# The gate products of a two-MLP attention kernel in Strassen's form

## The chip, the cores and the metric

The kernel runs on one core of a Trainium2 chip. The metric is device time in microseconds of a whole execution. The profile is of one such execution; its own time stands in the table below, beside the median of the runs.

## The reference

Attention on 4 x 8 heads of 576 tokens and 64 columns, half of the heads with a plain window of 32, half with a window dilated by 4, is laid out as 2,304 tokens of 512 columns and goes through two MLPs:

```
h  = x @ w_in                     # 2304 x 512 @ 512 x 2048
y  = maximum(0.01 * h, h) @ w_out # 2304 x 2048 @ 2048 x 512
a  = y @ w1;  b = y @ w2          # 2304 x 512 @ 512 x 1024, twice
out = ((a * b) @ w3) @ w_out2     # 1024 x 1024, then 1024 x 512
```

The inputs are float64 arrays, passed as 64-bit words. The change concerns the two products `y @ w1` and `y @ w2`, their elementwise product and the last product.

## The kernel before

**Number form.** Every matmul operand is kept as two float32r parts, high and low, and a product is three matmuls of 128 x 128 weights (`mm3`, L118 to L122: low x high, high x low, high x high). `split` (L109 to L116) makes the parts: a cast on one engine, a subtraction on another. Weights come as 64-bit words; `Convert` (L170) loads 512 KB of them at a time, forms float32 words in five passes (`to_float32`, L144: a scaling on an engine of choice, two passes of ScalarE, a shift and a word sum of VectorE), and hands them to a finisher that splits them into a slot.

**Stages.** Attention fills `xs`. The first MLP runs in turns: `hidden_steps` makes one block of 128 hidden columns for a chunk of tokens (12 matmuls into a bank `ps_h`), the activation follows on ScalarE, `split` on VectorE (and GpSimd), and `project_steps` multiplies the block into four sums `ps_x` (12 matmuls), two turns later (`LAG = 2`, L897). There are 7 chunks of 16 turns, 112 in all; the last ones have 384 tokens. A finished chunk is copied from PSUM into `st_t` (L491) and stored to `x2_dram` (L579). Meanwhile `w3 @ w_out2` is folded into one matrix, 1024 x 512, kept in `wp_dram` (`fold_steps` L635, `store_steps` L644): 32 fold steps whose `w_out2` parts are stored once and read back.

**Order.** Up to turn 96 the order on every engine is written out by hand: `START` (L794) is read one letter at a time, each letter issuing one step (H, g, c, l: a hidden turn; J: its projection; digits and d: conversions of the fold; W: a fold step), `LOADS` names the load behind each L. What follows is issued by loops, and the tile framework orders it: of the instructions that its own timing model has ready on an engine, the one issued first goes first. So TensorE's order after turn 96 may differ from the loops', while waits and queues still hold each engine to the order found. All loads and stores are issued by the sync engine, in one queue.

**Gate and last product.** In the last chunk's 16 turns (L912 to L949) the 16 column blocks of w1 and w2 are converted and split into the 16 slots `win` that the first MLP's weights leave; the folded matrix is loaded and split into `wo` slots (`load_wp`, `split_wp`). Then (L960 to L970) y is taken in blocks of 256, 512, 512, 512 and 512 tokens. `gate` makes, for one block of 128 columns, both products (24 matmuls), copies the first out of PSUM, multiplies, and splits the result into a `p` slot. `final` multiplies 128 tokens of `p` with the folded matrix (24 matmuls of 512 columns) and stores 256 KB of the result; it is issued among the gate steps of the next token block. `split_y` prepares a block of y during the block before it.

PSUM has three tags: `acc`, two pairs of banks (`bank2`), `side`, two banks (`side_bank`), and `h`, two banks (`bank`).

Of the kernel before, what the change touches and what calls it, by code (L numbers as in the profile page):

```python
# [8 lines left out]
F32 = mybir.dt.float32  # L9
# [19 lines left out]
def tile_window_attention_two_mlps(  # L29
# [30 lines left out]
    TB = 512  # L60
    GATE = [(0, T % TB)] + [(t, TB) for t in range(T % TB, T, TB)]
    NCB = len(GATE)
# [105 lines left out]
    LAST_CONV = ("GAD",)  # L168
# [40 lines left out]
    win, wout, w12, wo2, wp = {}, {}, {}, {}, {}  # L209
# [443 lines left out]
    yf, ys, pr = {}, {}, {}  # L653

    def load_y(c):
        t0, n = GATE[c]
        t = (fin if c else first_y).tile([P, NC, n], F32, tag="yf", name=f"yf{c}", bufs=1)
        nc.sync.dma_start(t, x2_dram[:, t0 : t0 + n].rearrange("(e p) t -> p e t", p=P))
        yf[c] = t

    wpf = {}

    def load_wp(ib):
        t = late.tile([P, DM], F32, tag="wpf", name=f"wpf{ib}", bufs=2)
        nc.sync.dma_start(t, wp_dram[ib * P : (ib + 1) * P, :])
        wpf[ib] = t

    def split_wp(ib):
        t = wo_slot(f"wps{ib}")
        split(t[:, 0], t[:, 1], wpf.pop(ib), nc.scalar, nc.gpsimd)  # L670
        wp[ib] = t

    def split_y(c, cc):
        if cc == 0:
            ys[c] = (fin if c else first_y).tile(
                [P, 2, NC, GATE[c][1]], F32R, tag="ys", name=f"ys{c}", bufs=2 if c else 1
            )
        t = ys[c]
        split(
            t[:, 0, cc], t[:, 1, cc], yf[c][:, cc], nc.scalar,  # L680
            nc.gpsimd if cc % 2 else nc.vector,
        )

    def gate(c, i):
        y, n = ys[c], GATE[c][1]
        if c == i == 0:
            ps = [side_bank(f"ps_ab{c}_{i}_{m}") for m in range(2)]
        else:
            both = bank2(f"ps_ab{c}_{i}")
            ps = [both[:, m] for m in range(2)]  # L690
        for m in range(2):
            for cc in range(NC):
                mm3(
                    ps[m][:, :n], parts(w12[m, i], cc), parts(y, cc), cc == 0, cc == NC - 1
                )
        t = fin.tile([P, TB], F32, tag="a", name=f"a{c}_{i}", bufs=2)[:, :n]
        nc.scalar.copy(t, ps[0][:, :n])  # L697
        g = fin.tile([P, TB], F32, tag="ab", name=f"ab{c}_{i}", bufs=2)[:, :n]
        nc.vector.tensor_tensor(g, t, ps[1][:, :n], op=ALU.mult)  # L699
        gg = fin.tile([P, 2, TB], F32R, tag="p", name=f"p{c}_{i}", bufs=NI + 4)[:, :, :n]  # L700
        split(gg[:, 0], gg[:, 1], g, nc.scalar, nc.gpsimd)
        pr[c, i] = gg

    def final(c, tb, pieces=1):
        r0 = GATE[c][0] + tb * P
# [17 lines left out]
    with ExitStack():  # L723
# [40 lines left out]
        PAIR_AT = "VVKVKVKVKVKVKVKVKVKVKVVVKKVKKKKV"  # L764
# [13 lines left out]
        for f in range(NF + AHEAD):  # L778
# [29 lines left out]
            "d2d13L2Jg3L45c645lH60J1dg02cd1lLH23453L645Jg6clH01d0Jgd2c1lL23H453L645J6gclH01d02dJg"
            "3L1c45l2H6L345Jg6L0Lc1dlLH20L31d4gJ5c2l6L3LW4LW56HL0Wg1dc0J2Ll1L32dWL34L45656WWL01dW"
            "L02H1dL3L23L4gW5cl6JeLf4W5061dWL021dWL3L243LH5L6JgclW01dHL23L4gW05c61lJL2d3LWHL4gJ05"  # L810
            "c61l2dWiL3jHkLmWgclJeLf4H5061d2Wg3LcJlLWHL4gW05c61lJL2d3LHWgclJL4W5061dHL23LWgclJL4H"
            "5061d2Wg3cJlLWHeLf4gJ05c61l2dW3HLWgclJL4W56HLJgclWHL4gW5cl6JWHJgclWHWgclJefHJgclHJgc"
            "l"
# [3 lines left out]
            "yyyyyyyyyyzzzyyzzzzyyzzzzyyzzyzzyzyzyzyzzyzzzyzzyzzzzzzz"  # L817
# [91 lines left out]
        turn = len(begun["Hgcl"][-1]) - 1  # L909
        first = turn + 1  # L910
        for c, f0, f1 in runs:
            if first >= f1 - f0:  # L912
                first -= f1 - f0
                continue
            f0, first, f00 = f0 + first, 0, f0
            if c == NCH - 1:
                fold_es.close()
                first_es, first_y = pool("first", "right")
                late_es, late = pool("late", "right")

                def raw_last(i):
                    return late.tile([P, 512], U64, tag="raw", name=f"raww{i}", bufs=2)

                wr = {}

                def w_slot(i):
                    wr[i] = late.tile([P, 2, 512], I32, tag="wr", name=f"wr{i}", bufs=2)
                    return wr[i][:, 0]

                jobs = [  # L930
                    (load_cols, (w1, w2)[m], i, keep_cols(w12, (m, i), f"w{m + 1}_{i}"))
                    for i in range(NI)
                    for m in range(2)
                ]
                conv = Convert(jobs, raw_last, w_slot, lambda i: wr[i][:, 1], LAST_CONV)
                conv.fetch(2)
                load_y(0)
            for f in range(f0, f1):
                turn += 1
                mlp1(c, f, f00, f1)  # L940
                lagged()
                if c == NCH - 1:
                    conv.step()
                    if 2 <= f < 2 + NI:
                        load_wp(f - 2)
                    if 3 <= f < 3 + NI:
                        split_wp(f - 3)
                    if 11 <= f < 11 + NC:
                        split_y(0, f - 11)  # L949
        while todo:  # L950
            project(*todo.pop(0))
        conv.step()

        gs_es.close()
        xs_es.close()
# [51 lines left out]
```

## Time and profile before

| | |
|---|---|
| median of 3 runs | 856.58 us (852.99 to 859.01) |
| profiled execution | 854.51 us, of which the span from first to last instruction is 852.7 us |
| granted TensorE clock | 1.00 of full speed in every slice |
| TensorE (PE) busy | 839.7 us, 98% of the span, 5,778 matmuls |
| VectorE (DVE), ScalarE (ACT), GpSimd (POOL) | 342.9, 351.1, 200.5 us: 40, 41, 24% |
| moved by DMA | 103.58 MB, 121 GB/s over the span; packets 40% of the 16 engines' time |
| gate and last product | from about 551.6 us to 849.6 us |

Engine names in the rows are those in brackets; PEld is TensorE's weight load, SPq the sync engine's queue. A group line reads: line, engine, operation, out<-in, shapes, count, busy us, mean ns of one, idle time before, and what ended it. Matmul durations overlap; their price is the distance between starts.

### The profile page before, as it was taken

The page shows a single profiled execution, that of the slowest core. Times are in us where ns is not written, and L with a number is a line of the kernel's source. Part 1 is how long each engine was busy: PE and PEld are TensorE (multiplying, and loading weights), DVE is VectorE, ACT ScalarE, POOL GpSimd, SP SyncE. Part 2 cuts the span into 40 slices and gives each one's busy share as a digit, 9 for nine tenths or more (in the row PEclk, how much of TensorE's full clock was granted, in tenths as well). Part 3 has the DMA queues.
Part 4 walks back from the last instruction along what each step waited for, and adds up shares of the span by engine and source line. Part 5 has one row for each costly group of instructions (what it writes and reads, how often), then busy time and mean ns, then how long its engine had stood idle before and what let it go on. Part 6 is the DMA issues. An engine that isn't in the chain of part 4 may idle for free.

```text
span 852.7 us, 14709 instructions
## 1 busy us (share of the span) xinstructions
PE 839.7 (98%) x5778; PEld 771.0 (90%) x5778; DVE 342.9 (40%) x705; ACT 351.1 (41%) x884; POOL 200.5 (24%) x230
## 2 busy tenths in 40 slices
PE   8899999999999999999999999999999999999998
PEld 7799999999999999889999999998888888888887
DVE  4799995246355346443321478631020010000000
ACT  4899874124545456453221465442121122111111
POOL 3210110132323234322221334142131131111110
PEclk9999999999999999999999999999999999999999
DMA  6985977134364037896643464141001000000001
GB/s 144 273 279 168 260 182 181 47 83 112 86 155 105 20 105 281 324 328 235 213 158 100 151 194 155 56 139 60 13 6 64 18 13 13 26 12 13 25 13 49
DMA packets 87332, 103.58 MB, mean 121 GB/s; under 512 B 42848, under 2 KB 65632, under 8 KB 87264
## 3 DMA queue, kind: packets, MB, share of 16 engines
q1 hardware_dynamic: 87264, 102.65, 39.8%
q8 instruction: 45, 0.74, 0.4%
q14 instruction: 23, 0.19, 0.1%
HBM read 85.72 MB, written 16.91 MB: 120 GB/s over the span
## 4 chain that ended last, share of the span: by engine, by line
PE 90%; DMA 4%; SPq 2%; DVE 1%; issue 1%; ACT 1%; POOL 0%; ACTq 0%; POOLq 0%; DVEq 0%
PE ps_h L120 8%; PE ps_x L120 8%; PE ps_x L122 7%; PE ps_x L121 7%; PE ps_ab L120 7%; PE ps_ab L121 7%; PE ps_ab L122 7%; PE ps_h L122 7%; PE ps_h L121 7%; PE ps_y L121 4%; PE ps_y L122 4%; PE ps_y L120 4%; PE ps_s L380 2%; PE ps_wp L120 2%; PE ps_wp L121 2%; PE ps_wp L122 2%
## 5 line engine op out<-in xcount | busy, mean ns | idle before, releaser
L120 PE MATMUL ps_h<-x,win 128*128 128x384 f32 (+2 forms) x448 | 143.3, 320 | 0.2
L122 PE MATMUL ps_h<-x,win 128*128 128x384 f32 (+2 forms) x448 | 140.0, 312 | 0.0
L121 PE MATMUL ps_h<-x,win 128*128 128x384 f32 (+2 forms) x448 | 139.9, 312 | 0.0
L699 DVE TENSOR_TENSOR ab<-a,ps_ab 128x512 f32<-128x512 f32 (+1 forms) x40 | 25.4, 634 | 233.5 <-ACT a L697 224.2
L120 PE MATMUL ps_ab<-ys,w 128*128 128x512 f32 (+1 forms) x320 | 117.7, 368 | 0.2 <-DVE ab L699 0.2
L122 PE MATMUL ps_ab<-ys,w 128*128 128x512 f32 (+1 forms) x320 | 117.7, 368 | 0.0
L121 PE MATMUL ps_ab<-ys,w 128*128 128x512 f32 (+1 forms) x320 | 117.6, 368 | 0.0
L120 PE MATMUL ps_x<-gs,wout 128*128 128x384 f32 (+2 forms) x356 | 114.1, 321 | 0.0
L122 PE MATMUL ps_x<-gs,wout 128*128 128x384 f32 (+2 forms) x356 | 112.4, 316 | 0.0
L121 PE MATMUL ps_x<-gs,wout 128*128 128x384 f32 (+2 forms) x356 | 112.3, 316 | 0.0
L505 ACT ACTIVATE g<-ps_h 128x384 f32<-128x384 f32 (+2 forms) x112 | 49.1, 439 | 135.5 <-PE ps_h L122 116.2
L112 POOL TENSOR_TENSOR p<-ab,p 128x512 fp32r<-128x512 f32 (+1 forms) x40 | 47.0, 1177 | 210.7 <-ACT p L110 210.7
L112 POOL TENSOR_TENSOR gs<-g,gs 128x384 fp32r<-128x384 f32 (+2 forms) x64 | 58.4, 914 | 154.2 <-DVE gs L110 154.2
L120 PEld LDWEIGHTS ps_h<-x,win 128*128 128x128 f32 x448 | 84.5, 189 | 2.9 <-PE ps_o L454 0.2
L121 PEld LDWEIGHTS ps_h<-x,win 128*128 128x128 f32 x448 | 84.6, 189 | 0.6
L122 PEld LDWEIGHTS ps_h<-x,win 128*128 128x128 f32 x448 | 84.5, 189 | 0.0
L110 DVE CAST gs<-g 128x384 fp32r<-128x384 f32 (+2 forms) x89 | 34.3, 386 | 120.7 <-ACT g L505 101.6
L697 ACT COPY a<-ps_ab 128x512 f32<-128x512 f32 (+1 forms) x40 | 21.7, 544 | 137.4 <-PE ps_ab L122 137.4
L120 PEld LDWEIGHTS ps_ab<-ys,w 128*128 128x128 f32 x320 | 60.1, 188 | 10.7 <-DVE ab L699 0.6
L121 PEld LDWEIGHTS ps_ab<-ys,w 128*128 128x128 f32 x320 | 60.1, 188 | 10.1
L122 PEld LDWEIGHTS ps_ab<-ys,w 128*128 128x128 f32 x320 | 60.1, 188 | 9.9
L120 PEld LDWEIGHTS ps_x<-gs,wout 128*128 128x128 f32 x356 | 67.1, 189 | 1.4
(108 smaller groups left out, 1567.4 us busy)
## 6 DMA issues: line engine op xcount, KB each, us to landing
wo<-wo_dram SPq DMA_DIRECT2D x32, 512.0 KB
raw<-in_moe_w_in_dram SPq DMA_DIRECT2D x16, 512.0 KB
raw<-in_moe_w_out_dram SPq DMA_DIRECT2D x16, 512.0 KB
rawf<-in_moe_w_dram SPq DMA_DIRECT2D x16, 512.0 KB
raww<-in_moe_w_dram SPq DMA_DIRECT2D x16, 512.0 KB
q<-in_q_dram SPq DMA_DIRECT2D x48, 140.0 KB
k<-in_k_dram SPq DMA_DIRECT2D x48, 140.0 KB
v<-in_v_dram SPq DMA_DIRECT2D x60, 96.0 KB
```

The source lines that it names most:

```text
L110: copy_on(e_hi)(hi, src)
L112: e_lo.tensor_tensor(lo, src, hi.bitcast(F32), op=ALU.subtract)
L120: nc.tensor.matmul(ps, a[1], b[0], start=first, stop=False)
L121: nc.tensor.matmul(ps, a[0], b[1], start=False, stop=False)
L122: nc.tensor.matmul(ps, a[0], b[0], start=False, stop=last)
L380: nc.tensor.matmul(ps[j * QB : (j + 1) * QB, i - bl.start], qt[d, i * QB : (i + 1) * QB], kt[d, first_key(i, plain) : first_key(i, plain) ...
L505: nc.scalar.activation(g, ps, AF.Prelu, alpha=SLOPE)
L697: nc.scalar.copy(t, ps[0][:, :n])
L699: nc.vector.tensor_tensor(g, t, ps[1][:, :n], op=ALU.mult)
```

## The change

The tokens of y are taken as three pairs of chunks of 384. A pair's y is a 2 x 2 matrix of blocks: chunk by half of the 512 columns. For one block of 128 output columns the weights are one too: half of the 512 rows by w1 or w2. The four wanted blocks (a and b for both chunks) come from seven products of a sum or difference of y blocks with a sum or difference of weight blocks (Strassen's form, `TERMS`), each 6 matmuls of 384 columns where the direct form has 8 blocks of 6.

The weight sums of each column block (7 x 2 x 2 blocks of 128 x 128) are made once, right after conversion, split, and stored to `ws_dram`; those of blocks 0 to 2 also stay in `win` slots, those of 3 to 7 go through two staging slots. From then on every pair loads each block's sums anew, four slots (7 x 256 KB) per column block, up to four column blocks ahead. The conversion starts after turn 92 (the order string is four turns shorter and its steps are placed anew), its scaling is on ScalarE instead of GpSimd. The sums of y are made by VectorE and split, four of the first pair's before the MLP ends, the other three where the MLP's tiles were, those of later pairs among the final blocks. The split of the folded matrix moves into the first pair's gate steps. The six final blocks of a pair follow its eight gate steps instead of standing among the next ones.

```diff
-    TB = 512
-    GATE = [(0, T % TB)] + [(t, TB) for t in range(T % TB, T, TB)]
+    MT = 384
+    NPC = T // (2 * MT)
+    NM = 7
+    TERMS = (
+        (((0, 0), (1, 1), PLUS), ((0, 0), (1, 1), PLUS)),
+        (((1, 0), (1, 1), PLUS), ((0, 0),)),
+        (((1, 1),), ((1, 0), (0, 0), MINUS)),
+        (((0, 0), (0, 1), PLUS), ((1, 1),)),
+        (((0, 0),), ((0, 1), (1, 1), MINUS)),
+        (((1, 0), (0, 0), MINUS), ((0, 0), (0, 1), PLUS)),
+        (((0, 1), (1, 1), MINUS), ((1, 0), (1, 1), PLUS)),
+    )
...
-    LAST_CONV = ("GAD",)
+    LAST_CONV = ("AAD",)
...
+    ws_dram = tc.dram_tile([NI, P, NM * 4 * P], F32, name="ws_dram")
+    def load_ws(p, i, x):
+        t = ws_slot(win_p, "win", NF, i, x, f"ws{p}_")
+        src, n = ws_place(i, x)
+        nc.sync.dma_start(t.bitcast(F32).rearrange("p a b c d -> p (a b c d)")[:, :n], src)
+        ws[p, i, x] = t
+    def keep_word(i, m, own):
+        def finish(w, e_hi, e_lo):
+            word[m] = w.rearrange("p (c f) -> p c f", c=NC)
+            if m == 0:
+                return
+            for k in range(NM):
+                x = k // 2
+                if k % 2 == 0:
+                    t = ws_slot(*((win_p, "win", NF) if own else (late, "stage", 2)), i, x, "ws0_")
+                terms = [word[b][:, 2 * a : 2 * a + 2] for a, b in TERMS[k][1][:2]]
+                if len(terms) == 2:
+                    s = late.tile([P, 2, P], F32, tag="sum", name=f"sum{i}_{k}", bufs=2)
+                    nc.vector.tensor_tensor(s, *terms, op=TERMS[k][1][2])
+                    yield
+                else:
+                    s = terms[0]
+                yield from split_steps(t[:, k % 2, 0], t[:, k % 2, 1], s, e_hi, e_lo)
+                if k % 2 or k == NM - 1:
+                    dst, n = ws_place(i, x)
+                    nc.sync.dma_start(dst, t.bitcast(F32).rearrange("p a b c d -> p (a b c d)")[:, :n])
+                    if own:
+                        ws[0, i, x] = t
+        return finish
...
+    def sum_y(p, k):
+        terms = [yf[2 * p + a][:, 2 * b : 2 * b + 2] for a, b in TERMS[k][0][:2]]
+        if len(terms) == 2:
+            s = pre.tile([P, 2, MT], F32, tag="ysum", name=f"ysum{p}_{k}", bufs=1)
+            nc.vector.tensor_tensor(s, *terms, op=TERMS[k][0][2])
+        else:
+            s = terms[0]
+        t = (pre if k < 4 else fin).tile([P, 2, 2, MT], F32R, tag=f"ys{k}", name=f"ys{p}_{k}", bufs=1)
+        split(t[:, 0], t[:, 1], s, nc.scalar, nc.vector)
+        ys[k] = t
...
+    def gate(p, i):
+        def product(ps, k):
+            w = ws[p, i, k // 2][:, k % 2]
+            for cc in range(2):
+                mm3(ps, parts(w, cc), parts(ys[k], cc), cc == 0, cc == 1)
+            return ps
...
+        both = bank2(f"ps_m{p}_{i}_0")
+        e1 = copy(temp("e1"), product(both[:, 0, :MT], 0))
+        e2 = copy(temp("e2"), product(both[:, 1, :MT], 1))
+        both = bank2(f"ps_m{p}_{i}_2")
+        m4, m5 = product(both[:, 0, :MT], 2), product(both[:, 1, :MT], 3)
+        c21 = add(temp("c21"), e2, m4)
+        c11 = add(temp("c11"), e1, m4)
+        c22 = add(temp("c22"), e1, e2, MINUS, nc.gpsimd)
+        e5 = copy(temp("e5"), m5)
+        add(c11, c11, m5, MINUS)
+        m3 = product(side_bank(f"ps_m{p}_{i}_4")[:, :MT], 4)
+        c12 = add(temp("c12"), e5, m3)
+        add(c22, c22, m3)
+        add(c22, c22, product(side_bank(f"ps_m{p}_{i}_5")[:, :MT], 5))
+        add(c21, c21, c22, ALU.mult)
+        add(c11, c11, product(bank(f"ps_m{p}_{i}_6")[:, :MT], 6))
+        add(c11, c11, c12, ALU.mult)
+        for c, g in ((1, c21), (0, c11)):
+            t = fin.tile([P, 2, MT], F32R, tag="p", name=f"p{2 * p + c}_{i}", bufs=2 * NI)
+            split(t[:, 0], t[:, 1], g, nc.scalar, nc.gpsimd)
+            pr[2 * p + c, i] = t
...
+        OWN = NI // 2 - 1
+        conv = Convert(
+            jobs, late_tile("raw", U64, 2), late_tile("w", I32, 4), late_tile("r", I32, 2), LAST_CONV
+        )
+        conv.fetch(2)
+        for t in range(len(begun["Hgcl"][-1]), len(turns)):
+            c, f, f0, f1 = turns[t]
+            mlp1(c, f, f0, f1)
+            lagged()
+            left = len(turns) - t
+            if left > 3:
+                conv.step()
+            if left == 4:
+                late_es.close()
+                pre_es, pre = pool("pre", "right")
+                load_y(0)
+                load_y(1)
+            if left == 2:
+                sum_y(0, 0)
+                sum_y(0, 1)
         while todo:
             project(*todo.pop(0))
+        sum_y(0, 2)
+        sum_y(0, 3)
+        for es in (gs_es, xs_es, wo2_es, mlp_es):
+            es.close()
         fin_es, fin = pool("fin", "left")
+        def ask(p, i):
+            while asked[0] < NPC * NI and asked[0] < p * NI + i + NF // 4:
+                for x in range(4):
+                    load_ws(*divmod(asked[0], NI), x)
+                asked[0] += 1
+        for k in range(4, NM):
+            sum_y(0, k)
+        for p in range(NPC):
             for i in range(NI):
+                ask(p, i)
+                gate(p, i)
+                if p == 0:
+                    load_wp(i)
+                    split_wp(i)
+                if i == 1 and p + 1 < NPC:
+                    load_y(2 * p + 2)
+                    load_y(2 * p + 3)
+            for tb in range(2 * MT // P):
+                last = p == NPC - 1 and tb == 2 * MT // P - 1
+                final(2 * p + tb // (MT // P), tb % (MT // P), 2 if last else 1)
+                if p + 1 < NPC:
+                    for k in (tb, tb + 1) if tb == 2 * MT // P - 1 else (tb,):
+                        sum_y(p + 1, k)
```

The order string keeps its letters but for four hidden turns and four projections, which leave it, and two warm-up matmuls, which join it (35 instead of 33); conversions, loads and fold steps stand at other places among them, the first fold step about 4 us of TensorE work later and the last three with no turn between them.

## Rows read from the trace of the kernel before

**Rows 1.** Page, part 1: busy time, share of the span, instructions.

```profile
PE 839.7 (98%) x5778; PEld 771.0 (90%) x5778; DVE 342.9 (40%) x705; ACT 351.1 (41%) x884; POOL 200.5 (24%) x230
```

**Rows 2.** Stretches: length; PE, PEld, DVE, ACT, POOL busy (count); clock; DMA share, GB/s.

```profile
512.04:545.32 33.28, 33.28 (x194) 33.28 (x193) 25.23 (x41) 19.64 (x36) 10.76 (x13) 1.00 0.43 135
...
580.14:591.02 10.88, 10.88 (x50) 9.00 (x49) 1.11 (x2) 1.99 (x4) 2.03 (x2) 1.00 0.00 0
...
577.26:580.14 2.88, 2.88 (x25) 2.88 (x24) 0.42 (x1) 0.57 (x2) 0.73 (x1) 1.00 0.53 206
...
554.00:849.60 295.60, 295.39 (x1415) 249.03 (x1413) 34.16 (x49) 64.12 (x116) 59.11 (x48) 1.00 0.10 33
...
466.60:554.00 87.40, 87.40 (x502) 86.87 (x502) 55.13 (x90) 45.45 (x83) 26.51 (x30) 1.00 0.43 136
...
345.00:385.00 40.00, 37.96 (x205) 34.12 (x204) 17.09 (x31) 17.93 (x30) 10.34 (x13) 1.00 0.95 340
```

**Rows 3.** Groups by form, whole span, TensorE in the gate (one of three lines).

```profile
L122 PE MATMUL ps_ab<-ys,w 128*128 128x512 f32 x256 | 99.6, 389 | 0.0
...
L122 PE MATMUL ps_ab<-ys,w 128*128 128x256 f32 x64 | 18.1, 283 | 0.0
```

**Rows 4.** Groups by form, whole span: other engines, nearest to the new work.

```profile
L578 DVE COPY st<-ps_x 128x384 f32<-128x384 f32 x6 | 3.3, 551 | 4.0 <-PE ps_x L122 4.0
...
L578 ACT COPY st<-ps_x 128x384 f32<-128x384 f32 x6 | 2.9, 481 | 9.9 <-DVE st L578 7.2 <-DMA x_dram<-st 1.7 <-DVE wr L157 1.0
...
L112 POOL TENSOR_TENSOR gs<-g,gs 128x384 fp32r<-128x384 f32 x32 | 32.7, 1022 | 86.1 <-DVE gs L110 86.1
...
L112 DVE TENSOR_TENSOR x<-g,x 128x256 fp32r<-128x256 f32 x8 | 3.3, 417 | 0.0
...
L110 ACT CAST p<-ab 128x256 fp32r<-128x256 f32 x8 | 3.2, 406 | 5.4 <-DVE ab L699 5.4
```

**Rows 5.** Timeline, VectorE (DVE), GpSimd (POOL), ScalarE (ACT): start, duration, instruction.

```profile
511.23 1.31 POOL L112 TENSOR_TENSOR wps<-wpf,wps 128x512 fp32r<-128x512 f32 x1
...
511.31 1.51 DVE L141 TENSOR_SCALAR wr<-wr 128x512 int32<-128x512 int32 x1 [0.78 <-POOL wr L107]
...
513.57 0.35 DVE L110 CAST gs<-g 128x384 fp32r<-128x384 f32 x1
...
513.95 0.56 DVE L112 TENSOR_TENSOR gs<-g,gs 128x384 fp32r<-128x384 f32 x1
...
514.43 0.68 DVE L112 TENSOR_TENSOR w<-wr,w 128x512 fp32r<-128x512 f32 x1
...
541.52 0.43 DVE L141 TENSOR_SCALAR wr<-wr 128x512 int32<-128x512 int32 x1 [0.77 <-POOL wr L107]
...
564.80 0.42 DVE L699 TENSOR_TENSOR ab<-a,ps_ab 128x256 f32<-128x256 f32 x1 [0.81 <-POOL ys L112]
...
564.76 0.74 POOL L112 TENSOR_TENSOR p<-ab,p 128x256 fp32r<-128x256 f32 x1
...
515.15 0.80 ACT L151 ACTIVATE wr<-raww 128x512 f16<-128x512 f32 x1 [1.78 <-DVE w L112]
...
515.81 0.78 ACT L153 ACTIVATE wr<-raww 128x512 int16<-128x512 uint32 x1
```

**Rows 6.** Timeline at the hand-over: TensorE, sync queue (SPq), ScalarE.

```profile
554.02 0.28 PE L120 MATMUL ps_ab<-ys,w 128*128 128x256 f32 x1
...
553.92 0.34 SPq L579 DMA_DIRECT2D x_dram<-st  x1
...
555.93 0.48 ACT L578 COPY st<-ps_x 128x384 f32<-128x384 f32 x1 [0.26 <-DMA x_dram<-st]
```

**Rows 7.** Waits (us, times, longest): TensorE, whole span; then ScalarE, 466.6 to 554.0.

```profile
PE ps_wp L120 <- DMA wo<-wo_dram: 1.1, 1, 1.1
...
PE ps_wp L120 <- DVE w3T L112: 1.0, 1, 1.0
...
ACT wr L151 <- DVE w L112: 19.4, 13, 2.3
```

More of the change, by code (lines that the diff above doesn't have):

```diff
@@ L59, in tile_window_attention_two_mlps @@
     NCH = len(CH)
-    TB = 512
-    GATE = [(0, T % TB)] + [(t, TB) for t in range(T % TB, T, TB)]
-    NCB = len(GATE)
+    MT = 384
+    NPC = T // (2 * MT)
+    NM = 7
+    PLUS, MINUS = ALU.add, ALU.subtract
+    TERMS = (
[7 more added lines that the diff above has]
+    )
     SR = S // DILATION
@@ L684, in gate, with temp, copy, add @@
[L684 to L702, printed above, removed]
+    def gate(p, i):
[4 more added lines that the diff above has]
+            return ps
+        def temp(name):
+            return fin.tile([P, MT], F32, tag=name, name=f"{name}{p}_{i}", bufs=1)
+        def copy(t, a):
+            nc.scalar.copy(t, a)
+            return t
+        def add(t, a, b, op=PLUS, e=nc.vector):
+            e.tensor_tensor(t, a, b, op=op)
+            return t
+        both = bank2(f"ps_m{p}_{i}_0")
[19 more added lines that the diff above has]
+            pr[2 * p + c, i] = t
@@ L908, in tile_window_attention_two_mlps @@
         todo += turns[len(begun["J"][-1]) : len(begun["Hgcl"][-1])]
[L909 to L936, printed above, removed]
-                load_y(0)
[L938 to L949, printed above, removed]
@@ new lines, in tile_window_attention_two_mlps, with late_tile @@
+        fold_es.close()
+        late_es, late = pool("late", "right")
+        def late_tile(tag, dt, bufs):
+            return lambda i: late.tile([P, 512], dt, tag=tag, name=f"{tag}l{i}", bufs=bufs)
+        OWN = NI // 2 - 1
+        jobs = [
+            (load_cols, (w1, w2)[m], i, keep_word(i, m, i < OWN))
+            for i in [*range(OWN, NI), *range(OWN)]
+            for m in range(2)
+        ]
+        conv = Convert(
+            jobs, late_tile("raw", U64, 2), late_tile("w", I32, 4), late_tile("r", I32, 2), LAST_CONV
+        )
@@ new lines, in tile_window_attention_two_mlps @@
+        conv.fetch(2)
[7 more added lines that the diff above has]
+            if left == 4:
+                assert not conv.done and conv.made == len(jobs)
+                late_es.close()
+                pre_es, pre = pool("pre", "right")
+                load_y(0)
+                load_y(1)
+            if left == 2:
+                sum_y(0, 0)
+                sum_y(0, 1)
@@ L950, in tile_window_attention_two_mlps @@
         while todo:
             project(*todo.pop(0))
-        conv.step()
-        gs_es.close()
-        xs_es.close()
-        wo2_es.close()
-        late_es.close()
-        fin_es, fin = pool("fin", "left")
-        load_y(1)
-        for c in range(NCB):
-            for i in range(NI):
-                gate(c, i)
-                if c > 0 and 1 <= i < 1 + GATE[c - 1][1] // P:
-                    final(c - 1, i - 1)
-                if i >= NI - NC and c + 1 < NCB:
-                    split_y(c + 1, i - (NI - NC))
-            if c + 2 < NCB:
-                load_y(c + 2)
@@ L969, in tile_window_attention_two_mlps @@
-        for tb in range(TB // P):
-            final(NCB - 1, tb, 2 if tb == TB // P - 1 else 1)
-        for es in (fin_es, first_es, mlp_es, wo_es, win_es):
+        sum_y(0, 2)
+        sum_y(0, 3)
+        for es in (gs_es, xs_es, wo2_es, mlp_es):
+            es.close()
+        fin_es, fin = pool("fin", "left")
+        asked = [OWN]
+        def ask(p, i):
[3 more added lines that the diff above has]
+                asked[0] += 1
@@ L972, in tile_window_attention_two_mlps @@
+        for es in (fin_es, pre_es, wo_es, win_es):
             es.close()
```

71 lines of the change are left out of this document (32 added, 39 removed).

## The prediction, made before the changed kernel ran

> **What bounds the kernel now.** I read the page's busy line first. TensorE is busy 839.7 us of a span of 852.7 us; VectorE, ScalarE and GpSimd are at 24 to 41% [rows 1]. The kernel ends when its matmuls end, so an edit is worth the matmul time it takes off, less the stalls it makes.
>
> Next, the table of stretches [rows 2]. Three of them are pure runs of one matmul width and give the start-to-start price, which is what counts; the mean durations of the groups [rows 3] overlap and are longer. Eight MLP turns of 24 matmuls of 384 columns fill 512.04 to 545.32: 33.28 / 192 = 0.1733 us each. One gate step of two sums of 24 matmuls has 48 of 512 columns in 10.88 us: 0.2267 us. Twenty-four of 256 columns take 2.88 us: 0.1200 us. (Their counts include a matmul or two that began before the edge.) The price is linear in columns: halfway between 0.1200 and 0.2267 is 0.1733. The gate and final stretch, 554.0 to 849.6, has TensorE busy 295.4 of 295.6 us: it has no slack to lose. The granted clock is 1.00 throughout.
>
> Then what feeds it. In the 87.4 us before the gate stage VectorE is busy 55 us, ScalarE 45, the DMA engines 43%; in the gate stage VectorE 34 of 296 us, DMA 10% [rows 2]. The new work goes into both stretches.
>
> **The products.** Before, each of 8 column blocks takes 24 matmuls over the 2,304 tokens, in four blocks of 512 and one of 256: 768 x 0.2267 + 192 x 0.1200 = 174.1 + 23.0 = 197.1 us; the groups show 3 x 256 and 3 x 64 [rows 3]. After: 3 pairs x 8 x 7 products x 6 matmuls = 1,008 of 384 columns, 174.7 us. **Gain 22.4 us.** An eighth of the columns goes, and 48 more matmuls take some of it back. The code fixes these counts, so there is no rival in which the work is not saved. The final products keep their 18 blocks of 24 matmuls: 0.
>
> **Emptying seven products.** A unit (one pair, one column block) now lasts 42 x 0.1733 = 7.28 us. VectorE has nine instructions of 384 columns, seven of them reading PSUM. The nearest row is the 384-column copy out of PSUM, 0.55 us [rows 4]; back to back, VectorE instructions start about 0.08 us sooner than the duration says (513.95, 0.56 us long, next start 514.43) [rows 5]. So 9 x 0.47 = 4.2 us, at most 9 x 0.55 = 5.0. ScalarE: three copies of 0.48 and two casts of about 0.5 (0.41 for 256 columns), 2.4 us. GpSimd: the difference and two low parts at 1.02 us [rows 4], 3.1 us. The split of the folded weight moves from the MLP into pair 0, with its eight 256 KB loads: a cast of ScalarE (under 0.8) and 1.31 us of GpSimd [rows 5] per unit, GpSimd then at 4.4. All stay under 7.28. The deepest wait is the last one, product seven to GpSimd's low part: add 0.55, multiply 0.56, cast 0.5, subtract 1.0, about 2.9 us with hand-overs. The final block behind it starts with column blocks 0 to 6, 21 x 0.2267 = 4.8 us of cover. Cost 0; were the cover gone, 3 x 3 = 9 us. Two pairs of PSUM banks and two side banks are each reused a unit later, after they have been emptied for 2 us or more: 0.
>
> One row speaks against this: VectorE's shift takes 0.43 us alone and 1.51 us when it starts beside a GpSimd subtraction, ending 0.28 us after that one ends [rows 5]. Two of the nine instructions (the multiplies) have both inputs in SBUF, as GpSimd has. With each held for a whole GpSimd instruction, VectorE needs 4.2 + 2 x 1.0 = 6.2 us, still below 7.28. The Trainium skill (SBUF — State Buffer, Who interferes with whom) says the same: such an instruction and a GpSimd one that reads SBUF exclude each other for the whole instruction, and one with at most one SBUF input doesn't contend. By that rule the seven PSUM readers are safe. The trace agrees: the 256-column gate multiply out of PSUM at 564.80 took 0.42 us with a GpSimd subtraction beside it all along [rows 5], no more than the usual 256-column subtraction [rows 4].
>
> **Weights from DRAM.** Each unit reads 7 x 256 KB = 1.84 MB, 21 of 24 times, behind 16 slots, four units. A unit's load starts when the unit four before it is done and has three units, 21.8 us, and the final blocks of each pair (6 x 5.44 = 32.6 us) load nothing but fetch up to four units ahead. So only four loads fall inside a pair's 58 us: unit 7 arrives at 7.3 + 4 L + 2, needed at 51. L may be 10.4 us, 176 GB/s. The dense stretch 345 to 385, where just such 512 KB blocks are read back, moves 340 GB/s at a share of 0.95 [rows 2]: L = 5.4. Pair 0 also loads two 768 KB token blocks and the fold, about 13 MB in 51 us, 250 GB/s. Bounds 0 and 5 us; I take 0. The sync queue gets four issues of 0.3 us a unit; what waits there for a slot holds back only later loads and stores.
>
> **The MLP's tail.** The changed order string has 92 hidden turns instead of 96; the fold is squeezed accordingly, by 4 x 4.16 us, and 20 turns with 22 projections, 42 x 2.08 = 87.4 us, are left. Into them go the 16 conversions and, new, the sums. Per column block: VectorE two shifts and two word sums (0.35 + 0.60 each, from 0.43 and 0.68) [rows 5], five sums and seven low parts of 256 columns at 0.34 (0.42 less 0.08) [rows 4], 6.0 us, and the MLP's own cast and subtraction, 2 x 0.8: 7.6 of 8.3 us. ScalarE: twice three passes at 0.66 (515.15 to 515.81) [rows 5], seven casts at 0.27 (0.41 less the same 0.14), the MLP's two activations at 0.34 (like the copy): 4.0 + 1.9 + 0.7 = 6.6. GpSimd loses the 16 scalings and the fold split, so nothing stretches VectorE here. DMA: 1.05 MB in and 1.84 MB out per block, 8 x 2.9 = 23 MB, and 1.5 MB of tokens: 25 MB in 87 us = 285 GB/s where 340 was reached. It fits, but the three are 80 to 92% full, where before they were at 63, 52 and 43% [rows 2].
>
> The tight spot is the staging: blocks 3 to 7 are summed into two slots, each freed when its 512 KB store has landed. The nearest row is a 192 KB store issued at 553.92 whose slot ScalarE takes at 555.93, 2.0 us [rows 6]. For 512 KB between 2.9 (2.0 and 0.33 MB more at 340 GB/s) and 7.5 us (three such blocks ahead of it, 1.54 each); a block's sums then take 4.2 us of VectorE and one landing, 7.1 to 11.7 us, against 8.3 us. I take 4 us, near the store row, as a store is the like operation: 8.2 us, just kept up with. The Trainium skill (DMA: Bandwidth & Descriptors, Anatomy of one DMA) fits a copy, for another issuing path, as 2.0 us plus its bytes at 436 GB/s: an estimate of 3.2 us for 512 KB, by which the staging keeps up and the sum stays; the 192 KB store, 2.0 us against its 2.5, was quicker. ScalarE's cast waits for the slot, and behind it in the queue the MLP's activation; TensorE allows about 5.7 us there: the PSUM bank is wanted three half turns of 2.08 later, less the activation's 0.5.
>
> **The hand-over.** Call the last projection's end T. The first four summed token blocks are prepared before T. Blocks 4 to 6 lie where the MLP's output staging was, and that is free when the last x2 store has landed: before, the fourth copy started at T + 1.9 (555.93, T = 554.02), so about T + 4.5 with the copy (0.48) and a landing of 2.0 [rows 6]. Cast 0.7 and low part 0.9 (768 columns, scaled from rows of 384): block 4 at T + 6.2, where TensorE wants it at T + 24 x 0.1733 = T + 4.2; block 6, with one buffer for the sum, another 1.3 us late: 3.3 us. The scheduler may fill it with the next unit's first products: 0 at best. With conversions 5 to 10 us late, as much as that more. **Cost 4.5 us** (0 to 16), of which 1.2 is for lateness.
>
> **The order string.** It is another order with the same matmuls. TensorE's waits in the part now compressed are 1.1 us for a reload and 1.0 us for a transposed block [rows 7]; four turns less cover could double or triple them, and the first fold step comes one turn later, which could remove both. Bounds -2 and +4; I take +0.5.
>
> **Sum**, in the profiled execution: 854.5 (span 852.7 and 1.8 around it) - 22.4 + 0 + 0 + 4.5 + 0.5 = 837.1. That execution is 2.1 below the median of 856.6, so 839 us in terms of the median.
>
> **Rivals.**
> *The staging falls behind.* With the 7.5 us landing, five blocks lose 3.4 us each, 17 us; 9 us of room (87.4 less 12 for the tokens, less 8 x 8.3) leave 8 or 9: 839 + 9 = 848. For it: the DMA share nearly doubles against the old tail. Against: reloads and conversions ran at 340 GB/s with TensorE losing 2 us.
> *The tail serialises: slower than before.* If ScalarE's queue, waiting on staged stores, also holds back the next block's conversion, nothing overlaps: 11.7 and 4.0 of ScalarE's passes, 15.7 us a staged block, 5 x 15.7 + 3 x 8.3 = 103 us. There are about 75: 87.4 less 12 for loading two token blocks (1.5 MB, 6.6 us) and their first sums. 28 us late: 839 + 28 = 867. It decides from 13.5 us a block, where 17 us late spends the gain. For it: each queue keeps its order. Against: in the old tail ScalarE waits for VectorE 13 times, up to 2.3 us, and TensorE never pays [rows 7].
> *The gate becomes VectorE's.* All nine instructions stretched to 0.95 us, 8.6 us a unit: 24 x 1.3 = 31, 870. Only if GpSimd also holds up PSUM readers, against the 0.42 us row.
> *Everything is filled.* No stall at the hand-over: 834, or 832 with the early waits gone.
>
> **Numbers.** A measurement here can tell about 1%: below 848 is faster, above 865 slower. Forecast 0.62 (833 to 846), staging 0.17 (846 to 855), serial tail 0.07, VectorE gate 0.03, filled 0.11 (830 to 833). Faster: 0.62 + 0.11 + a little under 0.03 of staging = 0.75; slower: the two others, less what stays below 865, 0.09; within 0.16. The range 831 to 853 leaves out under 0.2: the two slow rivals, the far end of staging, the best of filled.
>
> **What would show it.** Right: 1,008 products at 0.173 us in runs without gaps of 7.28 us a unit; final blocks straight behind them; one gap of 2 to 6 us where the first products wait for the summed tokens; PSUM readers at 0.55 us; DMA share near 0.8 in the tail and 0.7 in the gate. Wrong: turns longer than 4.16 us before the gate (staging), units longer than 7.3 us (VectorE, reloads), waits of first products for weights, or more than 5 us lost in the compressed fold.

## The result: 1% slower, and where the forecast gain went

| | before | after |
|---|---|---|
| median | 856.34 us (852.99 to 859.01, 4 runs) | 864.97 us (864.14 to 865.87, 4 runs) |
| ratio, 95% interval | | 1.0103 (1.0065 to 1.0141) |
| profiled execution, span | 854.51, 852.7 us | 864.42, 862.6 us |

The forecast was 839 us, range 831 to 853: the wrong direction, and out of the range. First the page of the changed kernel, parts 1 and 2 (of the second, TensorE's granted clock in 40 slices of 21.6 us):

```profile
PE 831.8 (96%) x5830; PEld 785.7 (91%) x5830; DVE 467.8 (54%) x987; ACT 388.4 (45%) x981; POOL 216.3 (25%) x236
...
PEclk9999999999999999999999999969999999999999
```

Against [rows 1] TensorE is busy 7.9 us less and the span is 9.9 us longer, so 17.8 us more are idle; and in one slice, the 27th, the clock is down to six tenths. The matmuls were saved (the new products are 1,008), the time wasn't. The same is seen by stretches (columns as in [rows 2]): the MLP's tail, the hand-over, the gate and final stage.

```profile
464.00:555.00 91.00, 87.92 (x501) 86.21 (x499) 66.33 (x167) 59.08 (x128) 4.63 (x4) 1.00 0.76 266
...
555.00:565.00 10.00, 1.09 (x4) 0.47 (x3) 3.55 (x5) 2.60 (x4) 0.00 (x0) 0.77 0.98 368
...
555.00:860.00 305.00, 286.42 (x1466) 264.19 (x1464) 147.26 (x253) 87.97 (x170) 89.47 (x80) 0.97 0.50 166
```

Where TensorE was busy 295.4 of 295.6 us before [rows 2], it now has 18.6 of 305 us idle, 8.9 of them in the first ten; and the tail, without a gap before, is idle for 3.1 of 91 us. The hand-over row by row, TensorE in the timeline (start, duration, instruction, idle time before and what ended it):

```profile
554.88 0.34 PE L132 MATMUL ps_x<-gs,wout 128*128 128x384 f32 x1
563.82 0.69 PE L130 MATMUL ps_m<-ys,ws 128*128 128x384 f32 x1 [8.61 <-ACT ys L120]
...
565.62 0.52 PE L130 MATMUL ps_m<-ys,ws 128*128 128x384 f32 x1
565.94 0.52 PE L131 MATMUL ps_m<-ys,ws 128*128 128x384 f32 x1
```

TensorE stands 8.6 us, and then, up to 570.4 us, its matmuls of 384 columns start 0.32 us apart instead of 0.173. What it waits for is the first token sum, and the sync queue (start, time to the end of the row's last issue) shows why that is late:

```profile
508.32 1.01 SPq L145 DMA_DIRECT2D rawl<-in_moe_w_dram  x2
511.64 7.92 SPq L700 DMA_DIRECT2D ws_dram<-ws  x4
519.66 1.01 SPq L145 DMA_DIRECT2D rawl<-in_moe_w_dram  x2
522.99 6.42 SPq L700 DMA_DIRECT2D ws_dram<-ws  x4
529.50 1.02 SPq L145 DMA_DIRECT2D rawl<-in_moe_w_dram  x2
530.89 18.12 SPq L700 DMA_DIRECT2D ws_dram<-ws  x10
...
552.63 1.32 SPq L708 DMA_DIRECT2D yf<-x_dram  x2
```

A column block's two raw loads (L145) leave only when the four stores (L700) ahead of them have left, and those wait for sums. So the loads of one block follow those of another after 11.3 and 9.8 us, where the forecast had 8.2 and the tail has room for 8.3. ScalarE's waits from 476 to 550 us (total us, times, longest) are for these loads above all:

```profile
ACT rl L161 <- DMA rawl<-in_moe_w_dram: 10.0, 7, 3.3
```

This alone doesn't say whether the raw loads or the staging slots set the pace; the runs with more of either do. The last low part of a weight sum ends about 551. The token loads (L708) leave behind the last stores and land at 561.84, 9.2 us later, with weight reloads before and behind them and the DMA engines 98% busy.

In the gate stage, 540 to 860 us, these waits stand out (total us, times, longest):

```profile
ACT e L743 <- DVE c L747: 53.5, 22, 3.4
DVE c L747 <- POOL p L122: 53.4, 35, 5.1
POOL c L747 <- DVE c L747: 34.7, 7, 7.8
...
PE ps_m L130 <- ACT e L743: 7.1, 12, 2.3
```

The first three are the side engines waiting for one another in a circle: ScalarE for VectorE, VectorE for GpSimd, GpSimd for VectorE. TensorE is at the end of it, through ScalarE's copies out of PSUM. GpSimd's one difference in a unit shows the pace; the second pair's:

```profile
686.94 1.02 POOL L747 TENSOR_TENSOR c<-e,e 128x384 f32<-128x384 f32 x1 [4.63 <-DVE c L747]
694.59 1.02 POOL L747 TENSOR_TENSOR c<-e,e 128x384 f32<-128x384 f32 x1 [4.68 <-DVE c L747]
702.35 1.02 POOL L747 TENSOR_TENSOR c<-e,e 128x384 f32<-128x384 f32 x1 [4.80 <-ACT e L743]
710.43 1.01 POOL L747 TENSOR_TENSOR c<-e,e 128x384 f32<-128x384 f32 x1 [5.11 <-ACT e L743]
```

Units of 7.65, 7.76 and 8.08 us, where 7.28 was forecast. A whole round of eight units and six final blocks, from the first of these rows to the same unit of the third pair (782.85), takes 95.9 us, where 8 x 7.28 + 32.6 = 90.9 was forecast. The groups of the gate show that no single instruction is slow (busy, mean ns, idle before):

```profile
L747 DVE TENSOR_TENSOR c<-c,ps_m 128x384 f32<-128x384 f32 x96 | 49.5, 549 | 52.4 <-PE ps_m L132 39.7 <-ACT e L743 12.6
...
L747 DVE TENSOR_TENSOR c<-c,c 128x384 f32<-128x384 f32 x48 | 25.8, 568 | 0.2
```

VectorE's PSUM readers take the 551 ns of [rows 4] and the multiplies 568: durations as forecast or better. Only their order costs.

### The profile page after: what moved, and what is told of

It is laid out like the page before. It is cut to its first block, busy times and chain, and to the rows that moved or that the text cites. A ratio compares the mean times of both kernels' runs of the same rounds, so it can differ in the third digit from the quotient of the medians.

```text
span 862.6 us, 15588 instructions
## 1 busy us (share of the span) xinstructions
PE 831.8 (96%) x5830; PEld 785.7 (91%) x5830; DVE 467.8 (54%) x987; ACT 388.4 (45%) x981; POOL 216.3 (25%) x236
## 4 chain that ended last, share of the span: by engine, by line
PE 78%; DMA 6%; ACT 6%; DVE 5%; SPq 2%; issue 1%; POOL 0%; ACTq 0%; DVEq 0%; POOLq 0%
PE ps_m L130 7%; PE ps_x L130 6%; PE ps_m L131 6%; PE ps_h L130 6%; PE ps_m L132 6%; PE ps_x L131 6%; PE ps_x L132 6%; PE ps_h L131 6%; PE ps_h L132 6%; DMA rawl<-in_moe_w_dram 4%; PE ps_y L130 4%; PE ps_y L132 4%; PE ps_y L131 4%; PE ps_s L390 2%; DMA yf<-x_dram 2%; PE ps_wp L132 2%
## 5 line engine op out<-in xcount | busy, mean ns | idle before, releaser
L130 PE MATMUL ps_m<-ys,ws 128*128 128x384 f32 x336 | 116.0, 349 | 16.4 <-ACT ys L120 9.3
L131 PE MATMUL ps_m<-ys,ws 128*128 128x384 f32 x336 | 116.0, 345 | 1.6 <-DVE ys L122 1.6
L132 PE MATMUL ps_m<-ys,ws 128*128 128x384 f32 x336 | 112.2, 344 | 0.0
L120 DVE CAST gs<-g 128x384 fp32r<-128x384 f32 (+2 forms) x89 | 31.6, 356 | 110.6 <-ACT g L515 93.3
L130 PEld LDWEIGHTS ps_m<-ys,ws 128*128 128x128 f32 x336 | 65.0, 194 | 21.8 <-ACT e L743 11.0
L743 ACT COPY e<-ps_m 128x384 f32<-128x384 f32 x72 | 33.9, 480 | 100.8 <-DVE c L747 53.5
L747 DVE TENSOR_TENSOR c<-c,ps_m 128x384 f32<-128x384 f32 x96 | 49.5, 549 | 52.4 <-PE ps_m L132 39.7
L747 DVE TENSOR_TENSOR c<-e,ps_m 128x384 f32<-128x384 f32 x72 | 39.3, 550 | 59.8 <-POOL p L122 53.4
L130 PEld LDWEIGHTS ps_x<-gs,wout 128*128 128x128 f32 x356 | 67.1, 189 | 3.6 <-ACT st L588 2.2
L122 POOL TENSOR_TENSOR p<-c,p 128x384 fp32r<-128x384 f32 x48 | 51.3, 1087 | 73.2 <-ACT p L120 51.0
L131 PEld LDWEIGHTS ps_x<-gs,wout 128*128 128x128 f32 x356 | 67.2, 189 | 0.8 <-DVE gs L122 0.2
```

The lines of the kernel that those rows point to most:

```text
L120: copy_on(e_hi)(hi, src)
L122: e_lo.tensor_tensor(lo, src, hi.bitcast(F32), op=ALU.subtract)
L130: nc.tensor.matmul(ps, a[1], b[0], start=first, stop=False)
L131: nc.tensor.matmul(ps, a[0], b[1], start=False, stop=False)
L132: nc.tensor.matmul(ps, a[0], b[0], start=False, stop=last)
L743: nc.scalar.copy(t, a)
```

## Experiments

Three causes stood against each other: late token sums (from raw buffers or from staging slots), the wait of the second product for the first copy, and the circle of buffers. Ratios are to the kernel before, in the same set of runs.

**Second product ahead of the first copy.** Products 1 and 2 write the two halves of one bank pair; in the changed kernel the first copy stands between them.

```diff
-        e1 = copy(temp("e1"), product(both[:, 0, :MT], 0))
-        e2 = copy(temp("e2"), product(both[:, 1, :MT], 1))
+        m1, m2 = product(both[:, 0, :MT], 0), product(both[:, 1, :MT], 1)
+        e1 = copy(temp("e1"), m1)
+        e2 = copy(temp("e2"), m2)
```

> Only the order in which two steps are issued is changed: product one is multiplied before product zero is copied out of its pair of banks. Theory A (TensorE's product one waits for ScalarE's copy of product zero, 0.79 us in each of 24 units, because the copy is issued between two writes of one pair of banks): the wait on ScalarE goes, a unit falls from 8.07 to 7.3 to 7.4 us, the time from 865 to 847 to 852 us. Rival R (the unit is 8.07 us because sums wait for GpSimd's low parts, all temporaries being single): the unit stays at 7.9 to 8.1 us and the time at 862 to 866. The 8.6 us gap before the first product stays in both.

Measured: 867.5 us, ratio 1.0118 (1.0095 to 1.0141). Neither expectation held whole: the units that follow one another fall to 7.64 us, but the total doesn't fall. A round is 97.0 us: TensorE stops seldomer and longer, once for 4.4 us in the first pair, and behind that its matmuls start 0.32 us apart. So that wait by itself is not what costs 15 us. With this edit the circle stands free. One unit, GpSimd, VectorE and ScalarE (start, time to the end of the row's last instruction, and the wait before it):

```profile
699.23 1.02 POOL L747 TENSOR_TENSOR c<-e,e 128x384 f32<-128x384 f32 x1 [4.69 <-DVE c L747]
700.20 1.99 POOL L122 TENSOR_TENSOR p<-c,p 128x384 fp32r<-128x384 f32 x2
706.87 1.02 POOL L747 TENSOR_TENSOR c<-e,e 128x384 f32<-128x384 f32 x1 [4.68 <-DVE c L747]
```

```profile
701.25 0.56 DVE L747 TENSOR_TENSOR c<-e,ps_m 128x384 f32<-128x384 f32 x1 [2.17 <-POOL p L122]
702.22 0.56 DVE L747 TENSOR_TENSOR c<-e,ps_m 128x384 f32<-128x384 f32 x1 [0.41 <-POOL p L122]
703.38 0.55 DVE L747 TENSOR_TENSOR c<-c,ps_m 128x384 f32<-128x384 f32 x1 [0.60 <-ACT e L743]
...
704.31 1.48 DVE L747 TENSOR_TENSOR c<-c,ps_m 128x384 f32<-128x384 f32 x3
705.71 1.02 DVE L747 TENSOR_TENSOR c<-c,c 128x384 f32<-128x384 f32 x2
```

```profile
702.87 1.24 ACT L743 COPY e<-ps_m 128x384 f32<-128x384 f32 x3 [2.82 <-DVE c L747]
```

GpSimd forms c22 of the next unit (699.23) as soon as the multiply has read the old one, and only then the low parts of c21 and c11 (to 702.19). Those two buffers are single, so VectorE's first sums of the next unit (701.25, 702.22) wait for them. ScalarE's next copies (702.87) wait for those sums, VectorE's rest (703.38 to 706.7) for a copy, and GpSimd's next c22 (706.87) for the multiply: 3.0 + 0.65 + 0.5 + 3.5 us, 7.64 around.

**Four raw buffers instead of two**, if the conversions were late for want of loaded words.

```diff
-            jobs, late_tile("raw", U64, 2), ...
+            jobs, late_tile("raw", U64, 4), ...
```

> Only the raw weight words of the MLP's tail get four buffers instead of two. Theory B (the tail runs late because each pair of raw loads is asked for only when the pair before has been read, 11 us a column block): blocks take 8 to 9 us, the token loads start 8 us earlier or more, the 8.6 us gap before the first product falls below 3 us, the granted clock stays at 1.00 and the time is 845 to 853 us. Rival S (the two staging slots of the sums hold the tail, as the prediction's rival had it): the gap stays at 7 to 9 us and the time at 861 to 866.

Measured: 866.75 us, ratio 1.0118 (1.009 to 1.0145), TensorE idle 9.6 us at the hand-over, the token loads issued at 551.89. Raw buffers are not the cause. The trace says more: from 476 to 550 us ScalarE now waits for no raw load, but for staging slots instead, and as long (sync queue and ScalarE below it):

```profile
ACT ws L120 <- DMA ws_dram<-ws: 14.6, 8, 3.9
```

```profile
508.76 9.63 SPq L700 DMA_DIRECT2D ws_dram<-ws  x4
...
515.62 0.41 ACT L120 CAST ws<-sum 128x256 fp32r<-128x256 f32 x1 [3.88 <-DMA ws_dram<-ws]
```

The first of these stores, 256 KB issued at 508.76, frees its slot for the cast at 515.62, 6.9 us later; a 512 KB one, issued at 499.35, after 5.3 us. So two waits hold nearly the same pace: for loads that stand behind stores in the one queue, and for slots. Taking away the first leaves the second.

**Four staging slots instead of two.**

```diff
-  ... (late, "stage", 2)), i, x, "ws0_")
+  ... (late, "stage", 4)), i, x, "ws0_")
```

> Only the staging slots of the weight sums are four instead of two. Rival S: the gap before the first product falls below 3 us, 845 to 853 us. Theory B: the raw loads still set the pace, gap 7 to 9 us, 861 to 866 us.

> The kernel with four staging slots once more, now timed in rounds: 847 to 850 us and, against the kernel before, a ratio of 0.988 to 0.993, if staging is the cause of the late tail; 860 or more would make the single look an accident.

Measured: 848.23 us in one run; with repetition 849.63 us, ratio 0.9916 (0.9887 to 0.9946): 15 us below the changed kernel, and below the kernel before. The repeated run's sync queue:

```profile
502.98 0.38 SPq L145 DMA_DIRECT2D rawl<-in_moe_w_dram  x1
504.64 3.54 SPq L700 DMA_DIRECT2D ws_dram<-ws  x3
...
512.33 0.38 SPq L145 DMA_DIRECT2D rawl<-in_moe_w_dram  x1
...
520.53 0.38 SPq L145 DMA_DIRECT2D rawl<-in_moe_w_dram  x1
522.15 14.18 SPq L700 DMA_DIRECT2D ws_dram<-ws  x9
...
537.71 1.24 SPq L708 DMA_DIRECT2D yf<-x_dram  x2
```

Both waits are nearly gone: loads stand between the stores, ScalarE waits 3.6 us for loads from 476 to 550 us and for no slot. Blocks are 9.4 and 8.2 us apart (502.98, 512.33, 520.53), and the token loads leave 14.9 us earlier. TensorE's gap shrinks to 0.3 us, and no matmul runs at half pace:

```profile
551.69 0.34 PE L132 MATMUL ps_x<-gs,wout 128*128 128x384 f32 x1
552.32 0.44 PE L130 MATMUL ps_m<-ys,ws 128*128 128x384 f32 x1 [0.29 <-ACT st L588]
```

**Reordered products with four raw buffers**, two slots as in the change.

> Both edits, the order of copy and product and four raw buffers. If theories A and B both hold and don't overlap: 832 to 838 us, near the 839 that was predicted, TensorE busy in one stretch. If only A holds 847 to 852, if only B 845 to 853; if the gains share a cause, about 845.

Measured: 863.26 us, ratio 1.0071 (1.0044 to 1.0097), 9.6 us idle at the hand-over: neither edit helps much while the staging is late.

**The difference c22 on VectorE**, with four slots and reordered products: GpSimd keeps the low parts alone.

```diff
-        c22 = add(temp("c22"), e1, e2, MINUS, nc.gpsimd)
+        c22 = add(temp("c22"), e1, e2, MINUS)
```

> Four staging slots, product one ahead of the copy, and the difference of the first two products on VectorE instead of GpSimd. Theory L (a unit is a ring of single temporaries: GpSimd's difference and two low parts, VectorE's first two sums that wait for them, ScalarE's copy, four sums, two multiplies, and round again, 7.64 us with the order edit, 8.08 without): the ring loses GpSimd's 1.0 us, units take 7.3 to 7.4 us and TensorE sets them, 836 to 842 us. Rival V (VectorE itself limits the unit): a tenth instruction makes units 7.9 us or longer, 850 us or more.

Measured: 845.84 us, ratio 0.9879 (0.9844 to 0.9914), less than expected, though GpSimd's low parts show units of 7.21 us in the second pair:

```profile
681.11 1.99 POOL L122 TENSOR_TENSOR p<-c,p 128x384 fp32r<-128x384 f32 x2 [5.22 <-ACT p L120]
688.32 1.98 POOL L122 TENSOR_TENSOR p<-c,p 128x384 fp32r<-128x384 f32 x2 [5.22 <-ACT p L120]
```

The shorter circle is enough where the gate runs evenly. In the first pair, where the fold's split and the other token sums come in between, one unit still lost 4.9 us, and the clock fell behind it (0.69 for the matmul):

```profile
575.71 0.69 PE L130 MATMUL ps_m<-ys,ws 128*128 128x384 f32 x1 [4.88 <-DVE c L747]
```

**Two buffers for c11 and c21**, with four slots and reordered products; `wpf` has one buffer instead of two, to make room.

```diff
-            return fin.tile([P, MT], F32, tag=name, name=f"{name}{p}_{i}", bufs=1)
+            return fin.tile([P, MT], F32, tag=name, name=f"{name}{p}_{i}", bufs=2 if name in ("c11", "c21") else 1)
```

> Four staging slots, product one ahead of the copy, and two buffers for the two temporaries that GpSimd's low parts read (c11 and c21; the folded weight's load gets one buffer instead of two to make room). Theory L: the first sums no longer wait for the low parts, units take 7.3 to 7.4 us, 836 to 842 us. Rival V: units stay at 7.6 us, 846 to 849 us.

Measured: **834.76 us** (834.47 to 835.63), ratio **0.9747** (0.9718 to 0.9776), better than both kernels. Its page and its units:

```profile
PE 821.4 (99%) x5830; PEld 781.1 (94%) x5830; DVE 465.7 (56%) x987; ACT 385.3 (46%) x981; POOL 213.4 (26%) x236
```

```profile
678.10 1.02 POOL L747 TENSOR_TENSOR c<-e,e 128x384 f32<-128x384 f32 x1 [4.55 <-PE ps_m L132]
...
685.43 1.01 POOL L747 TENSOR_TENSOR c<-e,e 128x384 f32<-128x384 f32 x1 [4.37 <-ACT e L743]
```

7.33 us from 678.10 to 685.43; VectorE doesn't wait for GpSimd in this unit, and in the gate TensorE itself waits for 0.7 us in all. Busy time of the side engines is what it was (VectorE 465.7 against 467.8): nothing was taken off them but the waiting.

**Weight sums not loaded anew**, with four slots: only the first four column blocks' sums are ever in the slots, and every later unit multiplies with one of those, so its products are other ones.

> Four staging slots; of the weight sums only those of the first four column blocks are ever in use, the other 20 units read the same slots and no reload follows (the products are then those of other weights). Theory D (reloads are hidden, the prediction's cost of 0): 846 to 849 us, units of 8.08 us as with four staging slots. Rival: reloads or the DMA traffic hold units up: 840 us or less, units shorter than 7.9 us.

Measured: 844.85 us in a single run, between the two expectations: 4.8 us below four slots alone. The units of the second and third pair are the same with the reloads and without, 7.65 to 8.08 us; in the first pair the sixth and seventh are 7.15 us without, 7.65 and 8.08 with. So bandwidth doesn't set the later units; what the reloads cost in the first pair, up to 5 us, one run doesn't settle.

**Which of the two gate edits counts?** Four slots with the two buffers but the copy left between the products; and four slots with the reordered products alone.

> Four staging slots and a second buffer for the two sums c11 and c21 (the buffer of the last weights before the final product goes from two to one), with the copy left between the first two products. Theory L (the ring of single temporaries is what stretches a unit, and TensorE's wait for the first copy is only where the ring shows on TensorE): 834 to 838 us, units of 7.3 to 7.5 us, as with the products reordered too (834.8). Rival O (the wait for the copy costs 0.45 us a unit by itself, ring or no ring): 841 to 846 us, units of 7.7 to 7.9 us.

> Four staging slots and the second product ahead of the first copy, all sums with one buffer. Theory L: the ring of 7.64 us stays, so 846 to 850 us against 849.6 with four slots alone. Rival O (the copy's wait is a cost of its own): 838 to 844 us.

Measured: two buffers alone 840.16 us, ratio 0.9804 (0.978 to 0.9828); reordering alone 851.41 us, ratio 0.993 (0.9904 to 0.9955), no better than four slots alone. With both, 834.8. The circle is the limit: while it stands, removing the copy's wait gives nothing. TensorE then waits in fewer places, 10.7 us in all as with four slots alone, but the longest is this, behind which its matmuls fall to 0.32 us:

```profile
PE ps_m L130 <- DVE c L747: 4.7, 1, 4.7
```

Once the circle is cut, the order is worth 5 us more, so in part the second theory held too. Rounds are 91.8 us with the two buffers alone and 91.9 with both edits, so these 5 us lie in the first pair.

**Two slots again, under the best gate.**

> The kernel of 834.8 us (four slots, products reordered, two buffers for c11 and c21) with the staging put back to two slots. Theory S (two slots cost the MLP's tail and the hand-over some 15 us, whatever the gate does behind it; four slots alone took 865.0 to 849.6): 847 to 852 us, with TensorE idle for 8 to 10 us at the hand-over. Rival G (with a faster gate the lateness is partly caught up, the gate having been what the ring allowed): 838 to 844 us.

Measured: 851.14 us, ratio 0.9923 (0.9898 to 0.9948). Staging costs as much here as under the slow gate, 15 to 16 us; a faster gate doesn't catch it up. By the two profiles, spans 849.3 and 832.9: the MLP ends 3.4 us later, TensorE then stands 8.7 us instead of 0.5, and the gate behind it takes 4.8 us longer, with the clock at 0.92 from 565 to 590 us. Set side by side, matmul by matmul, all of these 4.8 us arise in the first 150: 11 of them start 0.32 us apart, 1.6 us in all, and the rest are stops, 1.8 us of them for token sums.

**TensorE kept busy at the hand-over.** The changed kernel with 44 matmuls nobody reads.

```diff
+        w, busy = ws[0, 0, 0][:, 0].rearrange("p a b c -> p (a b c)"), bank("busy")
+        for d in range(44):
+            nc.tensor.matmul(busy[:, :MT], w[:, :P], w[:, :MT], start=d == 0, stop=d == 43)
```

> The changed kernel with 44 matmuls of 384 columns added whose result nobody reads, put on TensorE between the MLP's last matmul and the gate's first, so that TensorE is busy for about 7.5 us of the 8.9 us in which it waits for the first y sums. The arithmetic of the output is as in the changed kernel. Theory C (the idle stretch lowers the granted clock, and the gate's first matmuls at 0.32 us in place of 0.173 us cost 4 to 7 us): 858 to 862 us, with matmuls of 0.17 us from the first unit on. Rival H (the first units wait for the y sums and the ring anyway, so that slow matmuls are hidden): 864 to 867 us.

Measured: 867.67 us (866.83 to 875.78), ratio 1.0146 (1.0097 to 1.0195). TensorE in the timeline (41 of the 44 stand in the gap):

```profile
555.68 7.27 PE L1012 MATMUL busy<-ws 128*128 128x384 f32 x41
565.08 0.44 PE L130 MATMUL ps_m<-ys,ws 128*128 128x384 f32 x1 [2.12 <-ACT ys L120]
566.07 0.69 PE L131 MATMUL ps_m<-ys,ws 128*128 128x384 f32 x1 [0.55 <-DVE ys L122]
566.56 0.52 PE L132 MATMUL ps_m<-ys,ws 128*128 128x384 f32 x1
```

The gate's matmuls fell to 0.32 us all the same, now behind 2.1 us of idling and, one matmul later, 0.55 us. The run therefore can't tell what the half clock costs; the time is near the second expectation, but not for its reason. Under the best gate the run before it tells: 1.6 of the 4.8 us.

## Why the prediction was wrong

**Products, -22.4 us: right to 4 us.** In the kernel of 834.8 us, from the first product (552.33) to the last matmul's start (829.43) it is 277.1 us, against 174.7 + 98.2 = 272.9 of matmul time at the forecast prices. The products start 0.176 us apart in the gate, not 0.173.

**The MLP's tail, "8.2 us a block, just kept up with": wrong, 14.5 us.** That is the span of the change less that with four slots, 862.6 - 848.1: the MLP ends 3.2 us later, TensorE stands 8.6 us instead of 0.3, and from the first product on 3.0 us more are lost. The step that failed is the sum of 4.2 us of VectorE and a landing of 4 us: it counted nothing else in the ring, took the landing from a single 192 KB store in a quiet queue [rows 6], and left 1.2 us for lateness. In the changed kernel the stores of one staged block follow those of another after 11.4 us (511.64, 522.99): the next loads leave behind such stores, and a block's last casts stand behind the conversion of those loads on ScalarE. With four raw buffers, which take that away, slots came free 5.3 and 6.9 us after a store's issue, and the time stayed. By its pace, and by the stop of 8.6 us, this is nearest to *the staging falls behind* (11.7 us a block, 8 or 9 us late, a chance of 0.17), which left out the longer MLP and what late token sums and the fallen clock cost behind the stop. *The tail serialises* had 15.7 us a block, which no run shows. That its 867 us is close to the 865 measured is luck: half of the loss arose in the gate.

**The hand-over, +4.5 us: its mechanism didn't matter.** With the staging on time TensorE waits 0.3 to 0.5 us before the first product, near the "0 at best" of the prediction. All the 8.6 us of the change come through the token loads, which leave behind the last stores, and bring the fallen clock, which the forecast didn't price.

**Emptying seven products, 0: wrong, 15.2 us** (848.1 - 832.9, four slots without and with the two gate edits). Each engine's busy time was added up and compared with 7.28 us, and the conclusion drawn that all stay under it. But the buffers between the engines are single, so the engines work in turn: the step had to follow one unit's values from engine to engine until a buffer came free, which gives 7.64 us, nearly all of it durations that stood in [rows 4, 5]. The sentence on PSUM banks, "reused a unit later", asked that of the banks and not of c11, c21 and c22. The wait of the second product for a copy out of the same bank pair was missed as well; with it units are up to 8.08 us.

**Interference on VectorE: within its bound, but hardly met.** The PSUM readers took 549 ns, and 551 where GpSimd was at work beside them. Of the 48 multiplies 46 ran while GpSimd stood waiting, at 551 ns; one that met GpSimd's split of the folded weight (579.64 to 580.92) was held up:

```profile
580.03 1.30 DVE L747 TENSOR_TENSOR c<-c,c 128x384 f32<-128x384 f32 x1
```

**The order string, +0.5: a gain instead.** Both waits of [rows 7] for the fold are gone from TensorE's list, which is the lower bound of -2.

**Weights from DRAM, 0: within its bounds** of 0 and 5, as far as the one run without reloads tells.

The sum: 837.1 forecast + 14.5 + 15.2 = 866.8, less 2.4 for what the rest did better, is the 864.4 of the profiled execution. The kernel with both faults removed ran at 834.7, in its profiled execution, against the 837.1. That it came so near is in part luck: the hand-over took 0.5 us instead of 4.5 and the order gave 2 us instead of costing 0.5, while the products took 4 us more.

## What to carry to other kernels

An engine at half its time can still set the pace: where temporaries have one buffer, follow one value around from engine to engine until its buffer is free, and compare that circle with the period, not the busy sums. A staging ring needs enough slots that the next sums don't wait for a store to land, and the landing is to be taken from a queue as busy as the one it will stand in. In one queue with the stores the loads are late too, and then the trace shows a wait for loads where more slots are the cure: more raw buffers only moved the wait. Two late chains can hide one another: here a gate edit alone showed nothing, and was worth 5 us once the ring was cut.

## What the runs showed of the hardware

The granted clock of TensorE went to its lower level (matmuls of 384 columns 0.32 us apart instead of 0.173 to 0.176, 1.2 instead of 2.4 GHz) after 8.6 us of idling, after 4.9 us, and also after 2.1 us behind 41 dense matmuls and, one matmul later, 0.55 us. After 0.3 us (four slots) and 0.5 us (the kernel of 834.8 us) at the same place it did not, nor in the changed kernel after 0.7 and 1.3 us of idling around 575 us. VectorE's readers of PSUM and ScalarE's copies kept their durations (549 and 480 ns) in the gate; a VectorE multiply with both inputs in SBUF took 1.30 us beside a GpSimd subtraction, 0.55 us otherwise. In the busy tail with four raw buffers, a store of 256 KB and one of 512 KB freed their slots 6.9 and 5.3 us after issue.
